# A second output bank, new cuts, a later kv product, and fp32 dummy products in a one-core attention and FFN kernel

## The chip, the cores and the metric

The kernel runs on one core of one Trainium2 chip. The metric is the device time of one execution in microseconds (us). Several executions are timed beside the kernel before on the same chip; the profile is of one of them. Engine names in the profile: PE is the matmul engine (PEld its weight loads), ACT is ScalarE, DVE is VectorE, POOL is GpSimd, SP issues most stores and transposes.

## The reference

```python
def _attn_ref(q, k, v, g_norm):                 # q, k, v: 8 x 8 x 576 x 64, fp32
    kv = np.einsum('bhsd,bhse->bhde', k, v)
    out = np.einsum('bhsd,bhde->bhse', q, kv)
    rms = np.sqrt(np.mean(out * out, axis=-1, keepdims=True) + 1e-06)
    return out / rms * g_norm

def _moe_ref(x, w_a, w_b, w_out):               # x: 4608 x 512; d_ff 1536
    return ((x @ w_a) * (x @ w_b)) @ w_out
```

x is the attention's output, token by token, the heads side by side. There are 8 batches of 576 tokens; the FFN works in 9 strips of 512 tokens.

## The kernel before

PE is the engine that has to be kept fed. Batch 0 is done first, then the attention of each later batch is woven into the FFN of the strip before it. Three places matter here.

Ahead of the first pair of heads, dummy products keep PE busy while q, k and v are on their way:

```python
    def dummy(n, i, cols=STRIP):                # STRIP = 512
        for _ in range(n):
            nc.tensor.matmul(P[:, i, 0:cols], lhsT=zeros[:, 0:128], rhs=zeros[:, 0:cols], start=True, stop=True)
    # ... casts of q, k, v ...
    dummy(10, 0)
    # ... transposes of q, pair 0 ...
    dummy(3, 7)
    # ... kv of pair 0 ...
```

In the output product of strip 0, batch 1 is woven in. Group 0 (128 tokens, 12 products) is done first; the other three groups are cut into six pieces of six products, and the four head pairs follow one another, a step each piece:

```python
    pieces = [(1, h1), (1, h2), (2, h1), (2, h2), (3, h1), (3, h2)]
    for n, (g, fcs) in enumerate(pieces):
        halves[0] = n > 0
        o_mm(0, g, O, fcs)                      # output products into bank O = 3
        if fcs is h2:
            o_out(0, g, O)                      # copy out and store, DVE and ACT in turn
        if 0 <= n - 2 < NP:
            A.pss(n - 2, SS)                    # PE: mean of squares; ACT: its root (rs)
            A.pst(n - 2, X[n % 2])              # DVE: scale into xt
        if 0 <= n - 1 < NP:
            A.x(n - 1, X[(n - 1) % 2])          # PE: product of kvb and qT
            A.psq(n - 1, X[(n - 1) % 2])        # ACT: square
        if n < NP:
            A.qtr(n, 2)                         # PE: transpose q
            A.kv1(n, 2)                         # PE: kv, into the same bank 2
            A.kv_out(n, P[:, 2, STRIP - D :])   # ACT: copy kv to kvb
            A.qtr_out(n, 2)                     # DVE: copy q transposed to qT
```

With `halves` a 128-column product is issued as two of 64 columns that run side by side; I count such a pair as one product. In strip 1 the kv of all pairs of batch 2 comes after unit `k0` and the token products (`tx`) at `x0`; a unit is eight products.

Of the kernel before, what the change touches and what calls it, by code (L numbers as in the profile page):

```python
# [8 lines left out]
FP32 = mybir.dt.float32  # L9
# [6 lines left out]
def kernel(  # L16
# [11 lines left out]
    nc = tc.nc  # L28
# [6 lines left out]
    FC = d_ff // 128  # L35
    NP = H // 2
    HF = S // 2
    STRIP = 512
# [10 lines left out]
    def sb(shape, dt, name):  # L49
        return pool.tile(shape, dt, name=name, tag=name)  # L50
# [41 lines left out]
    zeros = sb([128, STRIP], BF16, "zeros")  # L92
# [15 lines left out]
    P = psum.tile([128, 8, STRIP], FP32, name="P", tag="P")  # L108
    O = 3
# [49 lines left out]
    def product(o, lhsT, rhs, **kw):  # L159
        for r in (slice(0, D), slice(D, 2 * D)) if halves[0] else (slice(0, 2 * D),):  # L160
            nc.tensor.matmul(o[r], lhsT=lhsT[:, r], rhs=rhs, **kw)  # L161
# [186 lines left out]
    class Unit:  # L348
        n = 0
# [35 lines left out]
    def ab_bank():  # L385
        ab_banks.append(ab_banks.pop(0))
        return ab_banks[-1]
# [9 lines left out]
    def store(t0, t, e0, e1, eng=nc.sync):  # L397
        i = 0
        while i < 128:
            b, j = divmod(t0 + i, S)  # L400
            if b < EARLY:
                c, p = divmod(j, EP)
                n = min(128 - i, EP - p)
                r0 = b * S + EC * p + c
                o = out[r0 : r0 + EC * (n - 1) + 1 : EC, e0:e1]
            else:
                n = min(128 - i, S - j)
                o = out[t0 + i : t0 + i + n, e0:e1]
            eng.dma_start(out=o, in_=t[i : i + n, e0:e1])
            i += n  # L410
# [3 lines left out]
    def o_mm(s, g, i, fcs, e0=0, e1=d_model):  # L414
        for fc in fcs:
            product(
                P[:, i, e0:e1],
                abt[s % 2][fc][:, g * 128 : (g + 1) * 128],
                wo_t[:, fc, e0:e1],
                start=(fc == 0),  # L420
                stop=(fc == FC - 1),
            )

    def o_out(s, g, i):
        n = n_o[0]
        n_o[0] += 1
        t = o_sb[n % 4]
        if n % 2:
            nc.scalar.copy(t, P[:, i, :])  # L429
        else:  # L430
            nc.vector.tensor_copy(t, P[:, i, :])  # L431
        store(s * STRIP + g * 128, t, 0, d_model)

    def ffn_o(s, g, i=O, between=None):
        o_mm(s, g, i, range(FC // 2))
        if between:
            between()
        o_mm(s, g, i, range(FC // 2, FC))
        o_out(s, g, i)


    def dummy(n, i, cols=STRIP):
        for _ in range(n):
            nc.tensor.matmul(  # L444
                P[:, i, 0:cols], lhsT=zeros[:, 0:128], rhs=zeros[:, 0:cols], start=True, stop=True
            )

    def pair_src(src, p):
        return src[0, 2 * p : 2 * p + 2].rearrange("h (t c) d -> t h c d", c=EC)

    g_src = g_norm.rearrange("(u d) -> u d", u=1)
    nc.sync.dma_start(out=q32, in_=pair_src(q, 0))
    nc.scalar.dma_start(out=k32, in_=pair_src(k, 0))
    load_pair(0, 1)
    nc.vector.memset(zeros, 0.0)

    nc.sync.dma_start(out=v32[:, 0:1], in_=pair_src(v, 0)[:, 0:1])
    nc.scalar.dma_start(out=v32[:, 1:2], in_=pair_src(v, 0)[:, 1:2])
    nc.scalar.dma_start(out=g_row[:, 0:D], in_=g_src)
# [26 lines left out]
    X, SS = (4, 0), 6  # L486
# [4 lines left out]
    def by_token(t):  # L491
        return t.rearrange("p c (h d) -> p h c d", h=2)
# [2 lines left out]
    nc.scalar.copy(by_token(kc0), k32)  # L495
    nc.vector.tensor_copy(by_token(vc)[:, 0], v32[:, 0])
    nc.scalar.copy(by_token(vc)[:, 1], v32[:, 1])
    dummy(10, 0)
    t = P[:, 2, :].bitcast(BF16)[:, 0:S].rearrange("q (c t) -> q c t", c=EC)
    for c in range(EC):  # L500
        nc.tensor.transpose(t[:, c, :], qc[:, c, :], ident[0:EP, 0:EP])
    A.qtr_out(0, 2)
    dummy(3, 7)
    for c in range(EC):
        nc.tensor.matmul(
            P[:, SS, 0 : 2 * D],
            lhsT=kc0[:, c, :],
            rhs=vc[:, c, :],
            start=(c == 0),
            stop=(c == EC - 1),  # L510
# [10 lines left out]
    for p in range(1, NP):  # L521
        i = X[p % 2]
# [42 lines left out]


    A = Attn(1)
    h1, h2 = range(0, FC // 2), range(FC // 2, FC)

    nc.sync.dma_start(out=gate_d, in_=vt[1][0:1, H - 1, EC - 1, D - 1 : D])  # L570
    nc.sync.dma_start(out=g_all, in_=g_norm.partition_broadcast(128))
    transpose_q(2)
    ffn_o(0, 0, X[0])
    pieces = [(1, h1), (1, h2), (2, h1), (2, h2), (3, h1), (3, h2)]
    for n, (g, fcs) in enumerate(pieces):

        halves[0] = n > 0
        o_mm(0, g, O, fcs)
        if fcs is h2:
            o_out(0, g, O)  # L580
        if 0 <= n - 2 < NP:
            A.pss(n - 2, SS)
            A.pst(n - 2, X[n % 2])
        if 0 <= n - 1 < NP:
            A.x(n - 1, X[(n - 1) % 2])
            A.psq(n - 1, X[(n - 1) % 2])
        if n < NP:
            A.qtr(n, 2)
            A.kv1(n, 2)
            A.kv_out(n, P[:, 2, STRIP - D :])  # L590
            A.qtr_out(n, 2)
# [9 lines left out]
    def slot(A, s, n):  # L601

        kb = P[:, 7, :].rearrange("q (b p e) -> q b p e", b=2, e=D)
        if s == 1:
            k0, xs = 5, (6.5, 8, 9.5, 11, 12.5)
        else:
            k0, x0 = {2: (2, 3.5), 3: (4, 5.5), 4: (0, 1.5), 5: (4, 5.5), 6: (0, 1.5)}[s]
            xs = tuple(x0 + x for x in (0, 1.5, 2.5, 4, 5))

        k0, x0 = {1: (5, 6.5), 2: (1, 2.5), 3: (4, 5.5), 4: (0, 0.5), 5: (4, 5.5), 6: (0, 0.5)}[s]  # L610
        if n == k0 and s in (1, 2, 3, 5):
            halves[0] = s < 5
            two = [A] if s < 3 else [A, Attn(s + 2)]
            for i, a in enumerate(two):
                for p in range(NP):
                    a.kv(p, kb[:, i, p, :])
            for i, a in enumerate(two):
                (nc.scalar.copy if i else nc.vector.tensor_copy)(a.kvs, kb[:, i])  # L618
        m = n - x0
        if m == 0:  # L620
            A.tx(ab_bank())
        for c in range(LC + 1):
            if m == 1.5 * c:
                A.tsq(c)
            if m == (1, 2, 4, 5, 7)[c]:
                A.tss(c)
            if m == (1, 2, 4, 5, 7)[c] + 0.5:
                A.trs(c)
            if m == (1, 2, 4, 5, 7)[c] + 1.5:
                A.txt(c)  # L630

    for s in range(1, N_STRIP - 1):
        b = s + 1
        A = Attn(b) if b < B else None
        for n in range(FC + 4):
            amid = (lambda n=n: slot(A, s, n - 0.5)) if A else None
            if n >= FC:
                ffn_o(s, n - FC, ab_bank() if n % 2 else O, amid)
            elif s > 1 or n > 1:
                ffn_ab(s, n, amid)  # L640
            if A:
                slot(A, s, n)

            if s == 1 and n == 3:
                load_late(3)
            if b + 1 < B and n == (12, 4, 8, 5, 8)[s - 1]:
                transpose_q(b + 1)
            if b + 2 < B and n == (14, 10, 14, 8)[s - 1]:
                load_late(b + 2)
# [47 lines left out]
```

## Time and profile before

| | before |
|---|---|
| time, median of 6 (lowest to highest) | 312.69 us (312.36 to 313.13) |
| span of the profiled execution | 310.8 us |
| PE busy | 98% |
| first transposes of q | 5.55 us |
| first output product of strip 0 | 35.15 us |
| kvb product of pair 2 / of pair 3, batch 1 | 45.92 / 48.16 us |
| token products of batch 2 | 63.91 us |
| last matmul starts | 307.61 us |

The last five rows are start times of single matmuls, from the timeline and the trace's records. They cut the kernel into stages, so that one can see in which stage time went. PE is nearly always busy, so a stage gets shorter only where PE waits. The page's part 4, the chain that ended last by engine, says that for 12% of the span the chain ran through loads, the last of them v of batch 2, which landed at 60.65 us:

```profile
PE 79%; DMA 12%; POOL 7%; issue 1%; ACT 0%; POOLq 0%
```

### The profile page before, as it was taken

The numbers are of one execution on the slowest core, as the hardware profiler recorded it, in microseconds if no ns is written. First come the engines' busy times: TensorE is split into PE (matmuls) and PEld (weight loads), VectorE is DVE, ScalarE is ACT, GpSimd is POOL, SyncE is SP. The second block draws the span as 40 slices with busy tenths as digits, with TensorE's granted clock in tenths as the row PEclk, the third lists the DMA queues.
The fourth block names the chain that finished last, engine by engine and source line by source line (L and its number), as shares of the span: only waits on it lengthen the run. The fifth ranks groups of instructions, "written<-read, shape, count | busy, mean of one in ns | idle before, by whom it ended". The sixth has DMA issues, their size and how long they took to land.

```text
span 310.8 us, 6542 instructions
## 1 busy us (share of the span) xinstructions
PE 304.3 (98%) x2684; PEld 157.6 (51%) x2701; DVE 140.6 (45%) x235; ACT 117.0 (38%) x231; POOL 101.3 (33%) x123
## 2 busy tenths in 40 slices
PE   7899999999999999999999999999999999999996
PEld 3444476655555555555555555444444444444444
DVE  4544335458248603484386123752782143214321
ACT  3743255354255313551564034632651233123310
POOL 8954991093274630043646300221240000000000
PEclk9999999999999999999999999999999999999999
DMA  8999999999899999047998990073021200030002
GB/s 180 197 196 199 201 188 168 161 169 184 174 137 185 139 174 193 2 84 134 178 177 118 162 188 2 19 160 110 20 51 42 103 1 0 34 103 0 0 36 101
DMA packets 94403, 36.29 MB, mean 117 GB/s; under 512 B 64934, under 2 KB 89894, under 8 KB 94374
## 3 DMA queue, kind: packets, MB, share of 16 engines
q0 software_dynamic: 59120, 18.44, 56.6%
q1 hardware_dynamic: 34786, 16.93, 25.0%
q10 hardware_dynamic: 468, 0.51, 0.6%
q8 instruction: 21, 0.34, 0.5%
q14 instruction: 8, 0.07, 0.1%
HBM read 37.78 MB, written 12.98 MB: 163 GB/s over the span
## 4 chain that ended last, share of the span: by engine, by line
PE 79%; DMA 12%; POOL 7%; issue 1%; ACT 0%; POOLq 0%
PE P L161 77%; DMA wb_t<-in_moe_w_b_dram 6%; DMA vtl<-in_v_dram 4%; DMA wo_t<-in_moe_w_out_dram 2%; PE P L293 1%; PE P L178 1%; POOL vt L119 1%; POOL qt L119 1%; POOL qs L142 1%; POOL kt L119 1%; POOL wa_t L477 0%; POOL wb_t L477 0%; POOL wo_t L134 0%; POOL ktl L145 0%; POOL vtl L145 0%
## 5 line engine op out<-in xcount | busy, mean ns | idle before, releaser
L377 DVE TENSOR_TENSOR ab<-P,asb 128x512 bf16<-128x512 f32 x108 | 74.4, 691 | 103.2 <-PE P L161 99.9
L161 PE MATMUL P<-xt,wb_t 128*64 128x512 bf16 (+1 forms) x641 | 111.4, 379 | 0.2
L161 PE MATMUL P<-xt,wa_t 128*64 128x512 bf16 (+1 forms) x636 | 111.0, 379 | 0.6 <-issue 0.2
L373 ACT CAST asb<-P 128x512 bf16<-128x512 f32 x108 | 63.1, 586 | 89.6 <-PE P L161 89.5
L161 PE MATMUL P<-wo_t,ab 128*64 128x512 bf16 (+3 forms) x673 | 95.5, 371 | 0.3
L161 PEld LDWEIGHTS <-ab 128*64 128x64 bf16 (+1 forms) x678 | 47.5, 106 | 45.0
L161 PEld LDWEIGHTS <-wa_t 128*64 128x64 bf16 (+1 forms) x644 | 46.0, 106 | 46.2 <-issue 0.6
L161 PEld LDWEIGHTS <-wb_t 128*64 128x64 bf16 (+1 forms) x644 | 45.8, 106 | 45.8
L330 POOL TENSOR_TENSOR sqt<-rst,g_all 128x512 f32<-128x512 f32 (+1 forms) x24 | 25.0, 1046 | 83.0 <-ACT rst L323 83.0
L429 ACT COPY osb<-P 128x512 f32<-128x512 f32 x17 | 10.0, 586 | 70.2 <-PE P L161 60.2
L431 DVE COPY osb<-P 128x512 f32<-128x512 f32 x18 | 12.4, 691 | 44.9 <-PE P L161 40.4
L142 POOL DMA_DIRECT2D qs<-in_q_dram x12 | 19.8, 1654 | 0.7 <-issue 0.3
L314 DVE TENSOR_REDUCE sst<-sqt 128x8 f32<-128x512 f32 (+1 forms) x24 | 16.3, 680 | 1.7 <-ACT sqt L310 1.5
L339 DVE TENSOR_TENSOR qv<-P,sqt 128x512 bf16<-128x512 f32 x18 | 12.3, 681 | 0.0
L330 POOL TENSOR_TENSOR k_x<-rst,g_all 128x512 f32<-128x512 f32 x6 | 6.3, 1044 | 17.4 <-ACT rst L323 17.4
L323 ACT ACTIVATE rst<-sst,eps_t 128x8 f32<-128x8 f32 (+1 forms) x30 | 9.0, 300 | 7.2 <-DVE sst L314 7.0
L310 ACT ACTIVATE sqt<-P 128x512 f32<-128x512 f32 x18 | 10.5, 585 | 0.1
L243 DVE SCALAR_TENSOR_TENSOR xt<-P,g_col,rs 128x288 bf16<-128x288 f32 x16 | 7.5, 511 | 5.1 <-ACT rs L233 5.1
L134 POOL DMA_DIRECT2D wo_t<-in_moe_w_out_dram x12 | 6.4, 530 | 6.7 <-DMA wb_t<-in_moe_w_b_dram 3.2
L233 ACT ACTIVATE rs<-P,eps_t 128x576 f32<-128x576 f32 (+1 forms) x9 | 6.1, 689 | 3.7 <-PE P L161 3.4
L139 POOL COPY gate<-qT 1x1 bf16<-1x1 bf16 x5 | 0.9, 177 | 18.9 <-DVE kvs L618 14.0
L444 PE MATMUL P<-zeros 128*128 128x512 bf16 x16 | 5.8, 510 | 1.2 <-DVE eps_t L461 1.2
(72 smaller groups left out, 131.7 us busy)
## 6 DMA issues: line engine op xcount, KB each, us to landing
out_dram<-osb SPq DMA_DIRECT2D x23, 256.0 KB, 2.1
qs<-in_q_dram POOLq DMA_DIRECT2D x12, 288.0 KB, 7.5
ktl<-in_k_dram POOLq DMA_DIRECT2D x6, 512.0 KB, 9.6
vtl<-in_v_dram POOLq DMA_DIRECT2D x6, 512.0 KB, 12.2
out_dram<-osb SPq DMA_DIRECT2D x13, 128.0 KB, 2.4
wo_t<-in_moe_w_out_dram POOLq DMA_DIRECT2D x12, 128.0 KB, 6.0
wa_t<-in_moe_w_a_dram POOLq DMA_DIRECT2D x5, 256.0 KB, 8.9
wb_t<-in_moe_w_b_dram POOLq DMA_DIRECT2D x5, 256.0 KB, 9.5
```

The source lines that it names most:

```text
L119: nc.gpsimd.dma_start(out=t[:, hs, :, :], in_=src[b, hs].rearrange("h (t c) d -> t h c d", c=EC))
L142: nc.gpsimd.dma_start(out=d[:, hs, :], in_=q[b, hs].rearrange("h t d -> t h d"))
L161: nc.tensor.matmul(o[r], lhsT=lhsT[:, r], rhs=rhs, **kw)
L310: nc.scalar.activation(sqt[c % 3][r], self.by_head(c)[r], AF.Square)
L314: nc.vector.reduce_sum(sst[c % 3][r], sqt[c % 3][r].rearrange("t j p d -> t (j p) d"), axis=mybir.AxisListType.X,)
L323: nc.scalar.activation(rst[c % 3][r], sst[c % 3][r], AF.Abs_reciprocal_sqrt, bias=eps_t[r], scale=1.0 / D,)
L330: nc.gpsimd.tensor_mul(sqt[c % 3][r].rearrange("t j p d -> t (j p) d"), rst[c % 3][r].unsqueeze(2).to_broadcast([n, H, D]), g_all[r].unsqu ...
L339: nc.vector.tensor_mul(t[r].rearrange("t (p j) d -> t j p d", j=2), self.by_head(c)[r], sqt[c % 3][r])
L373: nc.scalar.copy(self.t, self.a)
L377: nc.vector.tensor_mul(abt[self.s % 2][self.fc], self.b, self.t)
L429: nc.scalar.copy(t, P[:, i, :])
L431: nc.vector.tensor_copy(t, P[:, i, :])
```

## The change

The intent: kv of pairs 0 and 1 of batch 1 and kv of batch 2 wait for their v, so work is put ahead of them. For the second group to end within a piece it needs a bank of its own. The dummies become fp32, half as many.

```diff
+    zeros32 = zeros.bitcast(FP32)
+    def dummy32(n, i):
+        for _ in range(n):
+            nc.tensor.matmul(P[:, i, 0 : STRIP // 2], lhsT=zeros32[:, 0:128], rhs=zeros32, start=True, stop=True)
...
-    dummy(10, 0)
+    dummy32(5, 0)
...
-    dummy(3, 7)
+    dummy32(1, 7)
+    dummy(1, 7)
...
-    pieces = [(1, h1), (1, h2), (2, h1), (2, h2), (3, h1), (3, h2)]
-    for n, (g, fcs) in enumerate(pieces):
+    cuts = (12, 20, 27, 33, 36, 42, 48)
+    for n, cut in enumerate(cuts[1:]):
         halves[0] = n > 0
-        o_mm(0, g, O, fcs)
-        if fcs is h2:
-            o_out(0, g, O)
+        for i in range(cuts[n], cut):
+            g, fc = divmod(i, FC)
+            bank = X[1] + 1 if g == 1 else O
+            o_mm(0, g, bank, (fc,))
+            if fc == FC - 1:
+                o_out(0, g, bank)
...
-        k0, x0 = {1: (5, 6.5), ...
+        k0, x0 = {1: (5.5, 6.5), ...
```

## The prediction

> **What bounds the kernel now.** I read the page first, then the chain of work that ended last, then the timeline of PE (matmul), ACT (ScalarE) and DVE (VectorE) in the stretches that the change touches.
>
> The page's busy times and slices:
>
> ```profile
> PE 304.3 (98%) x2684; PEld 157.6 (51%) x2701; DVE 140.6 (45%) x235; ACT 117.0 (38%) x231; POOL 101.3 (33%) x123
> ...
> PE   7899999999999999999999999999999999999996
> ```
>
> PE is busy for 98% of 310.8 us and every slice but the first, second and last is full. So only time that PE spends waiting can be won, and it has to be searched in the start times of single matmuls, because a matmul's recorded end overlaps the next one's start. I compared each start with the start before it. A 512-column product is followed 0.216 us later when nothing holds it. Leaving out places where a record is missing (a double step every 10.8 us), the starts after 17 us lose more than 0.1 us in four places only, all in or just after the stage that the change rewrites (batch 1 woven into the output product of strip 0).
>
> The chain shows the last of the four:
>
> ```profile
> 47.20 13.45 DMA vtl<-in_v_dram
> 60.69 0.69 PE P L178 x32
> ```
>
> The second half of v of batch 2 lands at 60.65; kv of batch 2 (line 178) began at 60.32, stopped after eight of its 40 matmuls, and went on at 60.69: 0.22 us lost. The timeline of PE shows the other three:
>
> ```profile
> 39.13 0.45 PE L202 MATMUL P<-ident,qt 96*64 96x96 bf16 x12
> 39.60 0.38 PE L178 MATMUL P<-vt,kt 96*64 96x64 bf16 x12
> ...
> 41.33 0.45 PE L202 MATMUL P<-ident,qt 96*64 96x96 bf16 x12
> 41.82 0.38 PE L178 MATMUL P<-vt,kt 96*64 96x64 bf16 x12
> 42.01 1.49 PE L161 MATMUL P<-wo_t,ab 128*64 128x512 bf16 x12
> 43.31 0.44 PE L161 MATMUL P<-sq,ones 128*64 128x288 bf16 x4
> 43.55 0.44 PE L161 MATMUL P<-qT,kvb 128*64 128x288 bf16 x4
> 43.80 0.45 PE L202 MATMUL P<-ident,qt 96*64 96x96 bf16 x12
> 44.05 0.38 PE L178 MATMUL P<-vt,kt 96*64 96x64 bf16 x12
> 44.24 1.49 PE L161 MATMUL P<-wo_t,ab 128*64 128x512 bf16 x12
> 45.54 0.44 PE L161 MATMUL P<-sq,ones 128*64 128x288 bf16 x4
> 45.92 0.44 PE L161 MATMUL P<-qT,kvb 128*64 128x288 bf16 x4
> ```
>
> From the transposes (line 202) to kv is 0.26 us for pair 2 (43.80 to 44.05), but 0.47 for pair 0 and 0.49 for pair 1: kv waits for v of its pair. The trace's landing records put v of pairs 0 to 3 of batch 1 at 39.56, 41.78, 44.01 and 46.22, and kv started at 39.60, 41.82, 44.05 and 46.42. So 0.19 + 0.21 us are lost there. The fourth is before the product with kvb at 45.92: it comes 0.38 after the mean product at 45.54 where 0.25 is normal, so 0.11 with the exact starts. Its releaser stands in the timelines of ACT and DVE:
>
> ```profile
> 43.78 0.74 ACT L233 ACTIVATE rs<-P,eps_t 128x576 f32<-128x576 f32 x1 [1.01 <-PE P L161]
> 44.42 0.64 ACT L225 ACTIVATE sq<-P 128x576 bf16<-128x576 f32 x1
> 44.95 0.43 ACT L189 CAST kvb<-P 64x64 bf16<-64x64 f32 x2
> ```
>
> ```profile
> 45.42 0.45 DVE L209 COPY qT<-P 128x576 bf16<-128x576 bf16 x1
> ```
>
> ACT does the root of pair 0, the square of pair 1 and the copy of kv of pair 2 without a pause; DVE may copy qT of pair 2 only when that kv copy has ended (45.38), ends at 45.87, and PE goes on at 45.92. From the mean product of pair 0 (43.31) to the kvb product of pair 2 this chain takes 2.61 us.
>
> **What the Trainium skill says.** "PSUM — Partial Sum Buffer", PSUM bank collisions: two engines must not touch the same bank and quadrant at once. That is why DVE's qT copy stands behind ACT's kv copy, both in bank 2; the trace agrees (it starts 0.04 us after). "TensorE: Matmul & The Clock Gate", Part 1: PE starts at half clock and is released after a busy window of about 3.4 us. The trace agrees: the weight loads of the first dummies are 0.43 us apart up to 4.58 us, products later 0.216. "FP8 and Floating Point Precision", TensorE Precision Notes: a true fp32 product takes four passes. So 256 fp32 columns should cost what two 512-column bf16 products cost, and five replace ten exactly. The trace has one fp32 product only, of one column:
>
> ```profile
> 7.53 0.29 PEld L517 LDWEIGHTS P<-one,g_row 1*128 1x128 f32 x2
> ```
>
> It is recorded as two loads and two products. "TensorE: Matmul & The Clock Gate", Weight-path perf modes: the fast weight load doesn't work for fp32. The trace agrees as to direction: these loads last 182 ns, the bf16 loads of the dummies 95 to 151.
>
> **The change part by part.**
>
> Bank and cuts. The six pieces of 6 matmuls become 8, 7, 6, 3, 6, 6 (half-width pairs count as one). kv of pairs 0, 1, 2 moves later by 2, 3, 3 matmuls, that of pair 3 keeps its place (24 matmuls before it in both). The second group now ends in the middle of a piece, so the third must begin at once. In bank 3 it would have to wait for the second's copy (41.32 to 41.90); its own bank 1 avoids that. I see no collision in bank 1: it was read out before 35 us and is next needed by the products of pair 1 near 43.8. Step by step, with the durations of before:
> - Transposes of pair 0: 39.13 + 2 x 0.216 = 39.56. kv 0 at 39.85, v landed at 39.56: no wait.
> - kv 1: 39.85 + 0.19 (kv) + 7 x 0.216 + 0.25 (kvb product) + 0.28 (transposes) = 42.08, v landed at 41.78: no wait.
> - Mean product of pair 0: 42.08 + 0.19 + 6 x 0.216 = 43.56. Before: 43.31. It is 0.25 later: three matmuls more ahead of it (0.65) less two waits (0.39).
> - kvb product of pair 2: PE reaches it after 0.25 + 0.25 + 0.26 + 0.19 + 3 x 0.216 + 0.25 = 1.84 us. The chain through ACT and DVE still takes 2.61, since it starts at the same mean product and nothing in it is moved. PE waits 0.78 us (some 0.2 of it already at the mean product of pair 1, whose square ends 1.76 after the start). With six matmuls in that piece this wait was 0.11.
> - kv 3: 43.56 + 2.61 + 0.25 + 0.26 = 46.68, v landed at 46.22: no wait.
> - kvb product of pair 3: 46.68 + 0.19 + 1.30 + 0.25 = 48.41, before 48.16. Its own chain (square, kv copy, qT copy) ends near 48.15, so it adds nothing.
>
> Sum of this stage: +0.25 us, that is 0.78 - 0.11 - 0.19 - 0.21 = +0.27. The short piece takes back what the long ones gave: it removes exactly the work that covered the ACT chain.
>
> kv of batch 2. It moves by half a unit, four matmuls = 0.87 us, to about 61.44, after v has landed at 60.65: the 0.22 us go. Its copy to kvs then ends near 62.8; the product that needs it starts near 63.9. Free. The next load on the POOL queue waits for the DMA transpose that landed at 61.77, not for kvs as the wait table names it, so it doesn't move.
>
> Dummies. Ten at 0.43 (later 0.22) end their issue at 5.08 us; the first transposes wait for q until 5.55. So 0.47 us of room. Five fp32 products of four passes end at the same time: 0. One fp32 and one bf16 replace three, in 0.65 us, with room of 0.26 before k and v are cast (6.73): 0.
>
> Sum: +0.26 - 0.22 + 0 = about +0.04 us, on a median of 312.58: 312.6.
>
> **The rivals.**
> 1. The new wait isn't there (the ACT chain starts sooner, or PE doesn't need it as I think). Then the stage is bound by v of pair 3: kv 3 at 46.26 in place of 46.42, so -0.16, and -0.22 from batch 2: 312.2. For it: the cuts look chosen to meet the landings of v. Against it: the 0.11 us before 45.92 show the chain binding already with six matmuls.
> 2. The fp32 dummies are slower than ten bf16 ones. If each of ten half products also shows its weight load (0.11 us between the two loads above), the dummies end 1.1 later at most, less 0.47 of room: transposes up to 0.6 us late. The old kernel would have hidden 0.4 of it behind v; the new one doesn't. Against it: bf16 loads hide fully under running products. 312.9 to 313.2.
> 3. The clock is released at another moment. The profile had it full at 4.7 us, one window after the first dummy. If fp32 work counts as more, nothing is won, as the start waits for q and casts. If it counts as less, the release comes up to 3.4 us later and stretches the transposes, dummies and first kv (1.2 us of PE work), hence up to +1: 313.6. The three runs of before lie 0.56 apart, so such jitter may be in both kernels.
>
> **Range and chances.** The known terms are each under 0.8 us and cancel to 0.3 either way; run spread is 0.56. Prediction 312.6, range 312.0 to 313.3, with more room above for rivals 2 and 3. Two per cent is 6.3 us, ten times any term here: within 2% 0.98, 0.01 on each side.
>
> **What would show it right or wrong.** In the profile after: kv of pairs 0 and 1 some 0.28 after their transposes; the kvb product of pair 2 about 2.6 us after the mean product of pair 0, right after a DVE copy of qT, with 0.5 to 0.8 us of idle PE ahead of it and of the mean product of pair 1; kv of batch 2 in one run of 40 matmuls. It is wrong if that idle time is missing (rival 1), if the first transposes start later than 5.6 us (rival 2), or if products are still 0.43 apart after 5 us (rival 3).

## The result, and the profile after

| | before | after | |
|---|---|---|---|
| time, median of 6 | 312.69 us | 312.81 us (312.64 to 313.19) | ratio 1.0004 (0.9991 to 1.0017): same |
| span | 310.84 | 310.87 us | |
| first transposes of q | 5.55 | 5.63 us | +0.08 |
| first output product | 35.15 | 35.23 us | all before it +0.08 |
| kvb product of pair 3 | 48.16 | 48.44 us | stage +0.20 |
| token products of batch 2 | 63.91 | 63.95 us | stage -0.24 |
| last matmul starts | 307.61 | 307.65 us | stage 0.00 |

A ratio is the mean time of one kernel's fast runs over that of the other's fast runs of the same rounds, so it isn't quite the ratio of the medians quoted. The stages sum to +0.08 + 0.20 - 0.24 = +0.04 us.

The stage of batch 1 in the timeline of PE after (start, duration, engine, line, operation, out<-in, count):

```profile
39.64 0.45 PE L202 MATMUL P<-ident,qt 96*64 96x96 bf16 x12
39.92 0.35 PE L178 MATMUL P<-vt,kt 96*64 96x64 bf16 x12
...
43.61 0.41 PE L161 MATMUL P<-sq,ones 128*64 128x288 bf16 x4
...
44.54 0.82 PE L161 MATMUL P<-wo_t,ab 128*64 128x512 bf16 x6
45.40 0.44 PE L161 MATMUL P<-sq,ones 128*64 128x288 bf16 x4
46.21 0.44 PE L161 MATMUL P<-qT,kvb 128*64 128x288 bf16 x4 [0.37 <-DVE qT L209]
```

kv of pair 0 now follows its transposes after 0.28 us: its wait for v is gone. In its place stand two gaps. The short piece at 44.54 is three products = 0.65 us, so the mean product of pair 1 could follow at 45.20; it starts at 45.40. The kvb product of pair 2 could follow 0.25 later and starts at 46.21. Together 0.20 + 0.56 = 0.76 us, and the profile itself names DVE's copy of qT as the releaser. ACT and DVE in the same stretch:

```profile
44.06 0.74 ACT L233 ACTIVATE rs<-P,eps_t 128x576 f32<-128x576 f32 x1 [1.02 <-PE P L161]
44.70 0.64 ACT L225 ACTIVATE sq<-P 128x576 bf16<-128x576 f32 x1
45.23 0.43 ACT L189 CAST kvb<-P 64x64 bf16<-64x64 f32 x2
```

```profile
44.84 0.94 DVE L243 SCALAR_TENSOR_TENSOR xt<-P,g_col,rs 128x288 bf16<-128x288 f32 x2 [1.30 <-ACT rs L233]
45.70 0.46 DVE L209 COPY qT<-P 128x576 bf16<-128x576 bf16 x1
```

The root starts 0.46 us after the mean product of pair 0 (0.48 before), and each instruction follows the other at the distances of before; only PE gets there sooner. kv of batch 2 is one run of 40 without a gap (0.83 us in place of 1.07):

```profile
61.47 0.83 PE L178 MATMUL P<-vtl,ktl 128*64 128x64 bf16 x40
```

The trace's landing records put the last v of batch 2 at 59.23 us here, at 60.65 in the profile of before. The fp32 dummies:

```profile
1.19 4.28 PE L453 MATMUL P<-zeros 128*128 128x256 f32 x10 [1.19 <-DVE eps_t L470]
```

Five products are recorded as ten, 0.427 us apart at half clock (0.588 for the first step). And part 4 of the page:

```profile
PE 95%; DMA 1%; ACT 1%; DVE 1%; issue 1%
```

The waits for v are gone, yet the span is the same. The chain hardly runs through the loads any more, but that can't be put down to the change: on the page of fp32_only below, a kernel with the old cuts and the old place of kv, PE has 97% of the chain and loads have no part in it.

### The profile page after: what moved, and what is told of

The parts are those of the page before. It is cut to its first block, busy times and chain, and to the rows that moved or that the text cites. A ratio compares the mean times of both kernels' runs of the same rounds, so it can differ in the third digit from the quotient of the medians.

```text
span 310.9 us, 6538 instructions
## 1 busy us (share of the span) xinstructions
PE 304.2 (98%) x2682; PEld 158.6 (51%) x2699; DVE 140.7 (45%) x235; ACT 117.3 (38%) x231; POOL 101.7 (33%) x123
## 4 chain that ended last, share of the span: by engine, by line
PE 95%; DMA 1%; ACT 1%; DVE 1%; issue 1%
PE P L161 90%; PE P L178 2%; DMA qv<-in_q_dram 1%; PE P L293 1%; PE P L202 1%; PE P L216 0%; DVE xt L243 0%; ACT sq L225 0%; ACT rs L233 0%; PE P L444 0%; DVE qc L503 0%; PE P L453 0%; PE P L515 0%; PE P L510 0%; DVE qT L209 0%
## 5 line engine op out<-in xcount | busy, mean ns | idle before, releaser
L209 DVE COPY qT<-P 128x576 bf16<-128x576 bf16 x8 | 3.7, 457 | 5.8 <-ACT kvb L189 3.9
```

## The experiments

Eleven runs of ten kernels, each correct. The theory: in the stage of batch 1 the chain of root, square and kv copy on ACT, with scaling and qT copy on DVE, takes 2.6 us from the mean product of pair 0 to the kvb product of pair 2; the short piece uncovers it. The rivals: the wait has another cause; or the parts of the change do something else than that and cancel.

### cuts_only: bank and cuts alone

```diff
 (from the changed kernel)
-    dummy32(5, 0)  ...  dummy32(1, 7); dummy(1, 7)
+    dummy(10, 0)   ...  dummy(3, 7)
-        k0, x0 = {1: (5.5, 6.5), ...
+        k0, x0 = {1: (5, 6.5), ...
```

> Bank and cuts of the change alone; kv of batch 2 and the dummies as before. Chain theory: the mean product of pair 1 and the kvb product of pair 2 lose together 0.7 to 0.8 us, kv of pairs 0 and 1 lose nothing, and the kvb product of pair 3 stands 0.25 to 0.30 us later than in the kernel before, measured from the first output product. For batch 2 two readings. A: v of batch 2 lands at 60.6 as before, so the kv move was worth 0.2 us and this kernel is 0.2 us slower than the changed one (about 313.0). B: v lands near 59.2 as in the profile of the changed kernel, so kv doesn't wait at unit 5 either, and this kernel takes what the changed one takes (312.8).

Median 312.78 us against 312.62, ratio 1.0005 (0.9992 to 1.0017). The gaps at the mean product of pair 1 and the kvb product of pair 2 are the same to 0.01 us as in the changed kernel, so the cuts alone make them. From the first output product to the kvb product of pair 3 it took 13.20 us, 0.20 more than before (0.25 to 0.30 expected; before it was 13.00). For batch 2 neither reading held whole: v landed at 60.90, kv started at 60.69 and lost 0.10 us. The move is worth what the landing of v makes it.

### kv_only: kv of batch 2 half a unit later, alone

```diff
-        k0, x0 = {1: (5, 6.5), ...
+        k0, x0 = {1: (5.5, 6.5), ...
```

> Kernel before, with kv of batch 2 half a unit later and nothing else. Chain theory: the three small gaps of before (0.19, 0.21, 0.11 us) stay, kv of batch 2 runs its 40 matmuls without a gap, 0.1 to 0.25 us less: 312.45 to 312.6. Rival: v lands early in many executions and the 0.22 us of the profile of before were a chance of that run: no difference beyond 0.05 us in the time.

Median 312.53 us against 312.62, ratio 1.0002 (0.9988 to 1.0015): nothing that can be told from zero. kv of batch 2 ran without a gap, but v had landed at 60.30 in this execution, when the old place would have started kv at about 60.55 (61.42 - 0.87). Over the ten profiles with all dummies and the old place of the token products, v of batch 2 landed between 58.9 and 60.9 us. In the four profiles with kv at unit 5, kv lost 0.22 (before), 0.10 (cuts_only) and 0 us (fp32_only and tokens_early). The 0.22 is the upper end of a spread, so the rival is nearer to the truth than my theory.

A second part of the expectation failed. Of the three small gaps that I expected to stay, only the third did (0.38 us from 45.78 to 46.16, where 0.25 is normal). kv of pairs 0 and 1 didn't wait for v here, although the cuts are the old ones:

```profile
39.65 0.45 PE L202 MATMUL P<-ident,qt 96*64 96x96 bf16 x12
39.93 0.35 PE L178 MATMUL P<-vt,kt 96*64 96x64 bf16 x12
...
41.66 0.42 PE L202 MATMUL P<-ident,qt 96*64 96x96 bf16 x12
41.92 0.38 PE L178 MATMUL P<-vt,kt 96*64 96x64 bf16 x12
```

The first output product came at 35.67 us in this execution, 0.51 later than in the profile of before, and v of the two pairs landed at 39.66 and 41.88, before PE came to it. The profile of before has the earliest first output product of all thirteen profiles (35.15; the others with all dummies lie at 35.23 to 35.67), so its waits of 0.19 and 0.21 us are the long end of a spread too.

### fp32_only: the fp32 dummies alone

```diff
-    dummy(10, 0)   ...  dummy(3, 7)
+    dummy32(5, 0)  ...  dummy32(1, 7); dummy(1, 7)
```

> Kernel before, with the fp32 dummies alone. Neutral theory: first transposes at 5.5 to 5.65 us, set by the landing of q; full clock at about 4.6 to 5.1 us as in both profiles; time within 0.1 us of before (312.6 to 312.8). Rival: fp32 work is counted differently by the clock, the full clock comes more than 1 us earlier or later, and the time moves by 0.3 us or more.

Median 312.54 us against 312.62, ratio 1.0001 (0.9988 to 1.0014): neutral. The full clock came at 6.59 us here, 1.5 us later than the range that I gave, but over the eight profiles with fp32 dummies it came between 4.04 and 6.59, and with bf16 dummies at 4.71 (before), 5.16 (cuts_only) and near 5.9 (kv_only, which has no record of it: its first transposes start 62 and 59 ns apart and then 43, as at full clock). A spread of over 1 us is there with either; three profiles with bf16 are too few to show that the two are alike. The run shows one thing more. The first output product came 0.34 us later than in the profile of before (35.50), the kvb product of pair 3 only 0.07 us later (48.22). With the old cuts a late start is absorbed where kv waits for v: kv of pair 0 didn't wait here and kv of pair 1 only some 0.05 us. From the first output product to the kvb product of pair 3 it took 12.72 us here and 12.73 in kv_only, against 13.00 in before and 13.20 with the new cuts. So the new cuts cost 0.20 us against the profile of before and 0.47 against these two. With the new cuts a late start isn't absorbed: in cuts_only the same two were 0.17 late (35.32) and 0.36 late (48.52), that is 0.17 plus the 0.20 of the cuts.

### act_added: one more ACT copy in the chain

```diff
             A.kv1(n, 2)
+            if n == 2:
+                nc.scalar.copy(spare, zeros[:, 0:256])
             A.kv_out(n, P[:, 2, STRIP - D :])
```

> Changed kernel with one more ACT copy (128x256 bf16, from zeros to a spare tile) between the square of pair 1 and the kv copies of pair 2. If the ACT chain sets the wait of the kvb product of pair 2, that product comes later by what the copy adds between the square and the kv copy, 0.2 to 0.4 us: 2.8 to 3.0 us after the mean product of pair 0 in place of 2.60. The mean product of pair 1 stays at 1.79 after it. If DVE's scaling of pair 0 alone sets it, nothing moves.

One execution, 313.12 us. The timelines of ACT and of PE (the spare tile adds a line to the kernel, so line numbers are higher by one here and in dve_added):

```profile
45.33 0.41 ACT L605 COPY spare<-zeros 128x256 bf16<-128x256 bf16 x1
45.63 0.44 ACT L190 CAST kvb<-P 64x64 bf16<-64x64 f32 x2
```

```profile
45.50 0.44 PE L162 MATMUL P<-sq,ones 128*64 128x288 bf16 x4
46.61 0.44 PE L162 MATMUL P<-qT,kvb 128*64 128x288 bf16 x4 [0.68 <-DVE qT L210]
```

The kv copy starts 0.30 us after the added one, and the kvb product of pair 2 comes 2.90 us after the mean product of pair 0 (43.71) in place of 2.60: 0.30 more. The mean product of pair 1 stays at 1.79. So ACT's part of the chain has no room.

### dve_added: one more DVE instruction in the chain

```diff
             A.kv_out(n, P[:, 2, STRIP - D :])
+            if n == 2:
+                nc.vector.memset(spare, 0.0)
             A.qtr_out(n, 2)
```

> Changed kernel with one more DVE instruction (a memset of 128x256 fp32, 0.27 us) between DVE's scaling of pair 0 and its qT copy of pair 2. In both profiles the qT copy starts as soon as the second scaling lets DVE go and 0.04 us after ACT's kv copy: both ways are then equally long, and the kvb product of pair 2 comes 0.2 to 0.3 us later here (2.8 to 2.9 after the mean product of pair 0). If ACT alone sets it with room on DVE, it moves by less than 0.1.

One execution, 312.95 us. The timelines of DVE and of PE:

```profile
45.87 0.27 DVE L606 MEMSET spare<- 128x256 f32 x1
46.06 0.39 DVE L210 COPY qT<-P 128x576 bf16<-128x576 bf16 x1
```

```profile
46.51 0.44 PE L162 MATMUL P<-qT,kvb 128*64 128x288 bf16 x4 [0.59 <-DVE qT L210]
```

The kvb product comes 2.81 us after the mean product (43.70): 0.21 more. DVE has no room either. From the root on, the way over the square and the kv copy (ACT) and the way over the scaling (DVE) are equally long to some 0.06 us (of 0.27 us added, 0.21 came through). That shortening one of the two alone would gain next to nothing follows from this; no run tried it.

### same_bank: the second group in the common bank

```diff
-            bank = X[1] + 1 if g == 1 else O
+            bank = O
```

> Changed kernel with the second output group in the common bank again, everything else as changed. The third group's first product then waits for ACT's copy of the second: 0.7 to 0.9 us of idle PE within the second piece, after its fifth product. kv of the pairs behind it come that much later, so none waits for its v; the 0.74 us before the kvb product of pair 2 stays, as its chain starts later too. Time 0.7 to 0.9 us above the changed kernel: 313.5. Rival: the bank doesn't matter, since PE would have waited elsewhere anyway: no change in the time.

One execution, 313.60 us, 0.8 above the changed kernel's median; the stage from the first output product to the kvb product of pair 3 took 14.07 us, 0.87 more. PE in the second piece:

```profile
40.19 1.03 PE L161 MATMUL P<-wo_t,ab 128*64 128x512 bf16 x8
41.91 0.84 PE L161 MATMUL P<-wo_t,ab 128*64 128x512 bf16 x6 [0.68 <-ACT osb L429]
```

Between the starts of the fourth and fifth products lie 1.06 us in place of 0.22: 0.84 us of waiting for ACT's copy of the second group (I had expected it after the fifth, but group 1 ends with the fourth). The 0.76 us further on stay. So the bank of its own does what it is there for; without it the cuts would cost 0.8 us.

### mean_early: the chain started sooner

```diff
             g, fc = divmod(i, FC)
+            if n == 2 and i == cut - 4:
+                A.pss(0, SS)
+                A.pst(0, X[0])
...
-        if 0 <= n - 2 < NP:
+        if 0 < n - 2 < NP:
             A.pss(n - 2, SS)
```

> Changed kernel, with the mean product of pair 0 and its scaling issued four output products earlier (inside the third piece). Nothing else: the same work on each engine. Chain theory: the chain root, square, kv copy, qT copy starts 0.8 us earlier, the mean product of pair 1 and the kvb product of pair 2 lose less than 0.1 us together in place of 0.74; then kv of pair 3 arrives 0.4 us before its v and waits until 46.2 to 46.3 for 0.3 to 0.4 us; the kvb product of pair 3 starts 0.35 to 0.45 us earlier than in the changed kernel; time 312.4. Rival: the wait hangs on something else at that place (the copy of the third group's predecessor, a bank), and the kvb product of pair 2 starts where it did: no change.

Median 312.83 us against 312.62, ratio 1.0003 (0.9991 to 1.0016). The timelines of PE and ACT:

```profile
45.31 0.44 PE L161 MATMUL P<-sq,ones 128*64 128x288 bf16 x4
45.96 0.44 PE L161 MATMUL P<-qT,kvb 128*64 128x288 bf16 x4 [0.21 <-DVE qT L209]
```

```profile
44.44 0.65 ACT L225 ACTIVATE sq<-P 128x576 bf16<-128x576 f32 x1 [0.37 <-PE P L161]
```

The gap at the mean product of pair 1 is gone and the one before the kvb product fell from 0.56 to 0.40 us, so the chain is confirmed as the cause of that part: 0.36 of 0.76 us are away by nothing but an earlier start of it. I had expected less than 0.1 us to stay. What I had missed is that with the root out of the way ACT waits 0.37 us for PE, for the kvb product of pair 1 whose square comes next. The chain then hangs on that product. kv of pair 3 started at 46.46, not held by its v. From the first output product to the kvb product of pair 3 the stage took 12.87 us, 0.33 less than in the changed kernel. But the time didn't follow; 0.33 us is less than the half-width of the ratio's interval (0.4 us), so it could hardly have shown. In the profiled execution the gain was given back at 82 us, in the timeline of PE:

```profile
83.07 1.05 PE L161 MATMUL P<-xt,wa_t 128*64 128x512 bf16 x8 [0.36 <-DMA xt<-qv]
```

The first unit of strip 2 lost 0.52 us (start to start) to transposed tokens of batch 2, which landed at 82.93 us. In the profiles of before and of the changed kernel they landed at 81.25 and 81.66, when PE needed them at 82.75 and 82.79; in cuts_only they landed at 82.53.

### mean_early_again: a second profile of the same kernel

> The same kernel as mean_early, for a second profile and five more times. In the first the stage of batch 1 was 0.34 us shorter than in the changed kernel, but 0.52 us were lost at 82.3 us, where the first unit of strip 2 waited for the transposed tokens that a DMA landed at 82.93 us; in the profiles of before and of the changed kernel they landed at 81.25 and 81.66 for use at 82.75. Theory: that landing is chance (contention with the loads of batch 3 at that time), so here the wait is absent or different, and the stage of batch 1 is again 0.3 to 0.4 us shorter; median 312.4 to 312.7. Rival: the earlier start of strip 1 itself exposes it, and 0.3 to 0.6 us are lost there again; median 312.8.

Median 312.50 us against 312.57, ratio 1.0005 (0.9992 to 1.0017). Here the wait is absent:

```profile
82.57 1.03 PE L161 MATMUL P<-xt,wa_t 128*64 128x512 bf16 x8
```

The stage of batch 1 took 12.87 us again. The profiled executions took 312.98 and 312.42 us, and 0.52 of the 0.56 between them is that wait. The ten times of the kernel lie in two groups, five at 312.42 to 312.50 and five at 312.83 to 313.08; that the wait makes the upper group is shown for one execution of it only.

### tokens_early: tokens of batch 2 half a unit earlier

```diff
 (from mean_early)
-        k0, x0 = {1: (5.5, 6.5), ...
+        k0, x0 = {1: (5, 6), ...
```

> mean_early with kv of batch 2 at unit 5 again and the token products of batch 2 half a unit earlier (unit 6 in place of 6.5), so that the transposed tokens of strip 2 land 0.5 to 0.9 us earlier. The ten times of mean_early so far fall in two heaps, five at 312.42 to 312.50 and five at 312.83 to 313.08, and its two profiles, one of each heap, differ by the 0.52 us lost to those tokens at 82.3 us. If that is the cause of the upper heap, it empties here: all times 312.3 to 312.7, with up to 0.3 us lost to v of batch 2 at 60.4 us in its place where that lands late. If the upper heap stays (312.8 to 313.1 in two or more of the runs), its cause is another.

Median 313.13 us (312.78 to 313.58) against 312.84 on this chip, ratio 1.0007 (0.9994 to 1.0021). The wait at 82 us is absent in this profile, but 0.43 us were lost at 70.5 us, where a product waits for DVE, and the first output product came at 35.56, the second latest of the profiles with all dummies. So the upper group stays and the test doesn't tell why. On this chip the kernel before lay between 312.48 and 313.43 us, so the bounds of the two groups, taken on other chips, don't carry over to it either. No arrangement tried beats both kernels.

### half_bf16: half as many dummies without fp32

```diff
-    dummy32(5, 0)  ...  dummy32(1, 7); dummy(1, 7)
+    dummy(5, 0)    ...  dummy(3, 7)
```

> Changed kernel with half the dummies and no fp32: five bf16 products of 512 columns in place of five fp32 ones, then three as before the change. If an fp32 product of 256 columns really is worth two of these, these dummies end near 3.3 us, PE idles until q is cast at 5.6, the full clock comes a window[...] later or more, after 6 us, and kv of the first pair at 6.8 us is reached at half clock: 0.2 to 0.8 us more time. Rival: the number of instructions counts, not their length, and the full clock comes as early as with five fp32 products: same time.

Median 317.59 us (316.92 to 318.33) against 312.61, ratio 1.0166 (1.0151 to 1.0182): 5 us, against 0.2 to 0.8 expected. The direction was right, so length counts and not the number; that one fp32 product of 256 columns stands for two of bf16 is read from the trace of the changed kernel (two records of 0.427 us). The size was wrong. The full clock doesn't come one window later: products stay at half clock until about 17 us, and from the first transposes (6.16) to the first product of strip 0 (18.43) the stage takes 12.27 us in place of 8.55 (5.63 to 14.18) in the changed kernel. These 3.7 us are most of the 4.3 by which this execution (316.92) was longer than the changed kernel's profiled one (312.64); q landed 0.53 us later in it (5.52 in place of 4.99), and that is most of the rest.

### no_dummies: none ahead of the first pair

```diff
-    dummy32(5, 0)  ...  dummy32(1, 7); dummy(1, 7)
```

> Changed kernel without any dummy ahead of the first pair (neither fp32 nor bf16; those further on stay). Clock theory: PE does its first work at 5.6 us at half clock and is released [...]at 9 to 13 us; the stage to 14 us holds about 4 us of PE work with waits on ACT and DVE between, so it gets 0.5 to 1.5 us longer: 313.3 to 314.3. Rival: the stage is bound by the landing of q, k and v and by ACT and DVE, and the dummies buy less than 0.3 us, whatever their type.

Median 316.46 us (314.94 to 317.01) against 312.57, ratio 1.0110 (1.0088 to 1.0132): 3.9 us between the medians, 3.4 by the ratio, which leaves the slowest, profiled execution (317.01) out. I had expected 0.5 to 1.5 us and a release at 9 to 13 us. The busy times of the stage, first in this kernel and then in the changed one (length, then PE, PEld, DVE, ACT and POOL busy with counts):

```profile
5.60:17.80 12.20, 11.34 (x112) 5.84 (x112) 4.95 (x15) 5.19 (x9) 11.59 (x17) 1.00 1.38 198
```

```profile
5.60:14.10 8.50, 7.53 (x114) 4.63 (x117) 4.69 (x14) 5.05 (x9) 8.21 (x13) 1.00 1.34 197
```

DVE and ACT are busy for nearly the same time; PE's busy time grows from 7.53 to 11.34 us. These 3.8 us are most of the 4.4 by which this execution was longer than the changed kernel's profiled one. (The granted clock in the row, 1.00, is of no use here: the trace has no record before the release.) The release is recorded at 18.80 us. PE had been recorded busy for 93% of the 12.2 us up to 17.80 (the ends of matmuls are modelled), which didn't release it. Why not is open.

## Why the prediction was right

**The waits for v of pairs 0 and 1.** Right. kv 0 was predicted at 39.85 and kv 1 at 42.08; they started at 39.92 and 42.12, without a wait. The start-up came 0.08 us later (q was cast 0.07 later), which I couldn't have known, and it is in all absolute times. What the step had wrong is to take the waits of one profile, 0.19 + 0.21 us, as fixed: kv_only and fp32_only, with the old cuts, lost 0 and some 0.05 us there.

**The new wait.** Right, and it decided the case. Predicted 2.61 us from mean product to kvb product, 1.84 for PE to get there, 0.78 lost, 0.2 of it at the mean product of pair 1. Measured 2.60, 0.76 lost, 0.20 of it there. act_added and dve_added show that both the ACT and the DVE way set it (I had named ACT's kv copy alone as what DVE's qT copy waits for), mean_early that an earlier start takes half of it away. Rival 1 (no such wait, kv 3 held by v at 46.26) fell: kv 3 started at 46.71, predicted 46.68.

**The stage's sum.** Predicted +0.25 (its terms add up to +0.27 and the total takes +0.26; the rest is rounding), measured +0.20 us from the first output product to the kvb product of pair 3, that is +0.28 in absolute times with the start-up. That the sum fits is in part luck: it holds against the profile of before, from which the waits were read. Against kv_only and fp32_only it is +0.47.

**The bank.** Right: same_bank lost 0.84 us without it.

**kv of batch 2.** The amount was right by luck. I predicted that moving kv takes away the 0.22 us; the stage got 0.24 us shorter. But v landed at 59.23, and PE would have come to the old place at about 60.60 (61.47 - 0.87): kv wouldn't have waited there either. The step mistook a landing that differs by 2 us between executions for a fixed one. The four profiles with kv at unit 5 put the worth of the move at 0 to 0.22 us. With the cuts at +0.20 to +0.47, the change as a whole may cost some tenths of a us; the ratio, 0.9991 to 1.0017 or -0.3 to +0.5 us, can't tell this from zero.

**The dummies.** Right in effect. Four passes hold: each recorded half is 0.427 us at half clock. But the first weight load isn't hidden (0.588 us for that step), so the last half starts at 5.09 and the dummies end their issue at 5.31, not 5.08; that was within the 0.47 us of room. The single fp32 dummy further on takes 0.07 us more than I gave it (0.285 us for its first half), within its room too. Rival 2 (each load shows) fell: of the ten, all are hidden from the second half on. Its sign, first transposes later than 5.6 us, was met by the letter (5.63), but they waited for q and not for the dummies.

**The clock, rival 3.** It didn't happen in the profile after. In that of fp32_only the full clock came at 6.59 us, and kv of the first pair, right behind the last dummy, started at 7.06 in place of 6.81: 0.25 us. But as to the worst case I sized it wrong: "up to +1". A missed release costs 3.4 to 5 us (no_dummies, half_bf16), as the whole attention of batch 0 then runs at half clock. The chance of slower by over 2% rested on that size; even so, such a loss stays under 2% (6.3 us), though far outside my range.

## What to carry to other kernels

Work moved ahead of one wait is taken from another place; before moving it, ask which chain on the other engines that work was covering there, and time that chain from its first instruction to its last. A wait for a transfer seen in one profile is one draw: look at the landing, and at when the work that needs it arrives, in several executions before paying for its removal. Dummy products are to be judged by the stretch of time they fill, not by their number, and the price of one that is too short is paid in the whole stage behind it.

## What the Trainium skill lacked or had wrong

- "TensorE: Matmul & The Clock Gate", Part 1, says that what is issued in the first 3.4 us runs at 1.2 GHz and everything after at 2.4, and that the ramp costs under 1% of a typical kernel; its table asks for about 3.4 us of sustained work. Without dummies the release came at 18.80 us, 13 us after PE's first work and with PE recorded busy for 93% of the stage and for all of the 6 us from 12 to 18, and cost 1.1% (3.4 us); with dummies of 2.1 us it came near 17 us and cost 5 us. Part 4 of that page says that transposes don't count as busy in the same way; there are transposes in this stage, but no run here shows that they are the reason. With all dummies the ten recorded releases lie between 4.04 (tokens_early) and 6.59 us (fp32_only), a spread of 2.55 us, where Part 1 gives a variation of ±500 ns.
- "FP8 and Floating Point Precision", TensorE Precision Notes, gives the four passes of fp32, and no page gives the time of a whole fp32 product or says whether its weight loads hide. Here a 256-column fp32 product is two records of 0.427 us each at half clock, with the weight load hidden except in the first step (0.588 us), and at full clock 0.285 us after the first half and 0.216 after the second.
- No page says how much the landing of a load differs between executions: v of batch 2, with the same loads ahead of it, landed between 58.9 and 60.9 us in ten profiles.
